# A one-token attention kernel: uniform rolled loops, weights at the front of the DMA queue, and the output weights at its end in 4 KB rows

## The chip, the cores and the metric

The kernel runs on one core of one Trainium2 chip. The metric is the device time of one execution in microseconds (us). A time is the median of its runs.

The profile is one execution recorded by the hardware. PE is the tensor engine (PEld its weight loads), DVE the vector engine, ACT the scalar engine, POOL the general one, and SP the engine that issues DMAs. The profile shows 16 DMA engines, which share each large read: every 4 MB read counts up its semaphore in 16 increments.

## The reference

One query token attends to a cache of 65536 keys; beside it stands a small GELU feed-forward layer. Everything is bf16.

```python
xn  = layernorm(x)                                   # x: [1, 1, 512]
q   = (xn @ wq) -> 32 heads of 128                   # wq: [512, 4096], 4 MB
k,v = caches [8 kv heads, 65536, 128]                # 134 MB each; 4 query heads share one
o   = softmax(q k^T / sqrt(128)) v
out = x + o @ wo + gelu(xn @ w1 + b1) @ w2 + b2      # wo: [4096, 512], 4 MB; w1, w2 1.8 MB each
```

In all 280.5 MB must be read for 1 KB of result.

## The kernel before

K and V are read in 32 units each; a unit is 16384 keys, 4 MB, 32 KB in each of the 128 partitions, and each partition's 32 KB are contiguous in memory. There are four buffers ("slots") of 4 MB, two for K and two for V. For each K unit PE transposes 128 tiles into PSUM, DVE and ACT copy them out, and PE multiplies them with q ("scores"). ACT takes exponentials. PE then multiplies V's 128 tiles with the probabilities ("PV"). SP issues the next read of a slot as soon as PE is done with it. Here are the order of the reads and the emission of the programs; cuts are marked.

```python
chunks = [("K", 0), ("K", 1)]
for u in range(2, NU):
    chunks += [("K", u), ("V", u - 2)]
chunks += [("V", NU - 2), ("V", NU - 1)]
# after K0: four small loads and wq (into a V slot); after K1: w1, w2 (the other V slot)
# the last V goes in four pieces, then the wo rows of the last four heads:
LASTP = (64, 32, 16, 16)
...
def dma_wo_cur(k):            # two heads of wo at a time, one such load in each later pair
    sch.dma(SP, lambda: sp.dma_start(
        out=wo_cur[:, :, :],
        in_=A_wo[k * HW * DH:(k + 1) * HW * DH, :].rearrange("(h p) n -> p h n", p=128)),
        sem_misc, writes=["wo_cur"])        # a row of wo is 512 bf16: 1 KB
...
def pair(i):                  # two units; the first pair has special cases and stands unrolled
    ...
    scores(0, 1)
    v_block(ua - 2, 0)        # PV in four blocks between the scores
    scores(0, 2)
    v_block(ua - 2, 1)
    ...
@block.scalar
def _(e): _emit(e, ACT.ops)   # straight-line program
@block.vector
def _(e): _emit(e, DVE.ops)   # straight-line program
@block.tensor
def _(e): ...                 # PE: first pair straight, the other 15 in a loop, then the tail
```

Of the kernel before, what the change touches and what calls it, by code (L numbers as in the profile page):

```python
# [22 lines left out]
class _Eng:  # L23
    def __init__(self, name, sem, is_pe=False):
        self.name = name
        self.sem = sem
        self.count = 0
        self.clock = {}
        self.ops = []
        self.is_pe = is_pe  # L30
        self.deferred = []

# [11 lines left out]
class _Sched:  # L44
# [61 lines left out]
    def op(self, eng, fn, reads=(), writes=(), publish=True, inc=1):  # L106
        req = self._required(reads, writes)
# [43 lines left out]
def _fold(bodies):  # L151
# [13 lines left out]
    ops = []  # L165
    for k in range(len(bodies[0])):
        assert len({(b[k][2] or (None, 0))[1] for b in bodies}) == 1
        need = {}
        for (kk, s), at in seen.items():
            if kk == k:  # L170
                need[s] = max(v - i * growth[s] for i, v in at.items())
        ops.append((bodies[0][k][1], bodies[0][k][2], need))
    out = []
    known = {}
    for fn, pub, need in ops:
        waits = [(s, v) for s, v in need.items() if known.get(s) is None or known[s] < v]
        for s, v in waits:
            known[s] = v
        out.append((waits, fn, pub))
# [14 lines left out]
def _emit_loop(eng_obj, ops, growth, n):  # L194
# [7 lines left out]
    for s, vs in uses.items():  # L202
        key = (vs[0], growth[s]) if len(vs) == 1 else s
        if key not in regs:
            r = eng_obj.alloc_register(f"w{len(regs)}")
            eng_obj.reg_mov(r, vs[0])
            regs[key] = r
            steps.append((r, vs[0] + growth[s] - vs[-1]))
        at[s] = [regs[key], vs[0]]
    with eng_obj.Fori(0, n):  # L210
# [10 lines left out]
        for r, step in steps:  # L221
            eng_obj.reg_add(r, r, step)


def bass_parallel_sum__gqa_block_cached__dense_activation_gelu__decode_kernel(
# [31 lines left out]
    CW = TPD * HPG  # L257
    assert D % 128 == 0 and F % 128 == 0 and S % CKEYS == 0 and CPG == 4
    assert A_k_cache.shape[3] == DH and H % G == 0 and KT == 4 and HPG == 4
    assert KT * H * DH <= TPD * DH and KT * F + FC * D <= TPD * DH and CW <= 512  # L260

# [18 lines left out]
    ident_bf = nc.alloc_sbuf_tensor("ident_bf", [128, 128], BF)  # L280
    ident_f = nc.alloc_sbuf_tensor("ident_f", [128, 128], F32)
    ones_f = nc.alloc_sbuf_tensor("ones_f", [128, 128], F32)

    rows_bf = nc.alloc_sbuf_tensor("rows_bf", [2, D], BF)
    ones2_bf = nc.alloc_sbuf_tensor("ones2_bf", [2, 1], BF)
    xT_bf = nc.alloc_sbuf_tensor("xT_bf", [128, KT], BF)
    b1T_bf = nc.alloc_sbuf_tensor("b1T_bf", [128, FC], BF)
    xT_f = nc.alloc_sbuf_tensor("xT_f", [128, KT], F32)
    xsq = nc.alloc_sbuf_tensor("xsq", [128, KT], F32)
    st = nc.alloc_sbuf_tensor("st", [128, 2], F32)  # L290
    mom = nc.alloc_sbuf_tensor("mom", [128, 8], F32)
    xnT_bf = nc.alloc_sbuf_tensor("xnT_bf", [128, KT], BF)
    qT_bf = nc.alloc_sbuf_tensor("qT_bf", [128, H], BF)
    q_cur = nc.alloc_sbuf_tensor("q_cur", [128, HPG], BF)
    h_f = nc.alloc_sbuf_tensor("h_f", [128, FC], F32)
    g_t1 = nc.alloc_sbuf_tensor("g_t1", [128, FC], F32)
    g_t2 = nc.alloc_sbuf_tensor("g_t2", [128, FC], F32)
    gT_bf = nc.alloc_sbuf_tensor("gT_bf", [128, FC], BF)
    finT = nc.alloc_sbuf_tensor("finT", [128, KT], F32)
    fin_bf = nc.alloc_sbuf_tensor("fin_bf", [128, 128], BF)  # L300
# [3 lines left out]
    kv = nc.alloc_sbuf_tensor("kv", [128, NSLOT * TPD * DH], BF)  # L304
# [4 lines left out]
    w1_sb = kv[:, w1_at:w1_at + KT * F].rearrange("p (kt f) -> p kt f", kt=KT)  # L309
    w2_at = w1_at + KT * F  # L310
    w2_sb = kv[:, w2_at:w2_at + FC * D].rearrange("p (fc n) -> p fc n", fc=FC)
    kt_ring = nc.alloc_sbuf_tensor("kt_ring", [128, NKT * BCOL], BF)
    HW = 2
    wo_cur = nc.alloc_sbuf_tensor("wo_cur", [128, HW, D], BF)
    HT = HPG + HW
    wo_end = nc.alloc_sbuf_tensor("wo_end", [128, HT, D], BF)
    P_bf = [nc.alloc_sbuf_tensor(f"P_bf{i}", [128, CW], BF) for i in range(2)]
    P_v = [P_bf[i][:, :].rearrange("p (t j) -> p t j", j=HPG) for i in range(2)]

    pmax = nc.alloc_sbuf_tensor("pmax", [128, HPG], F32)  # L320
    gmax4 = nc.alloc_sbuf_tensor("gmax4", [HPG, 1], F32)
    diag4 = nc.alloc_sbuf_tensor("diag4", [HPG, HPG], F32)
    negm = nc.alloc_sbuf_tensor("negm", [128, NU * HPG], F32)
    sums = nc.alloc_sbuf_tensor("sums", [128, NU * HPG], F32)
    o_all = nc.alloc_sbuf_tensor("o_all", [128, NU * HPG], F32)
    nmin = nc.alloc_sbuf_tensor("nmin", [128, H], F32)
    coef = nc.alloc_sbuf_tensor("coef", [128, NU * HPG], F32)
    wtot = nc.alloc_sbuf_tensor("wtot", [128, NU * HPG], F32)
    rden = nc.alloc_sbuf_tensor("rden", [128, H], F32)
    o_c = nc.alloc_sbuf_tensor("o_c", [128, NU * HPG], F32)  # L330
    o_sum = nc.alloc_sbuf_tensor("o_sum", [128, H], F32)
    oT_cur = nc.alloc_sbuf_tensor("oT_cur", [128, HW], BF)
    oT_next = nc.alloc_sbuf_tensor("oT_next", [128, HW], BF)
    sums_cur = nc.alloc_sbuf_tensor("sums_cur", [128, CPG * HPG], F32)
    spare = nc.alloc_sbuf_tensor("spare", [128, 2], F32)
    oL_bf = nc.alloc_sbuf_tensor("oL_bf", [128, HPG], BF)
# [7 lines left out]
    PA_MOM = 48  # L344
    PA_SB = 56
    PA_AT = 72
    PA_FT = 80
# [3 lines left out]
    LASTP = (64, 32, 16, 16)  # L351
    LASTH = (HPG - 1, 1)
    assert sum(LASTP) == TPD
    lsem = [sch.dsem(f"lsem{i}") for i in range(len(LASTP))]
    csem = [sch.dsem(f"csem{i}") for i in range(NSLOT)]
    sem_misc = sch.dsem("dmisc")
    sem_wq = sch.dsem("dwq")
    sem_w12 = sch.dsem("dw12")
    sem_wo = sch.dsem("dwo")
    hsem = [sch.dsem(f"hsem{i}") for i in range(len(LASTH))]  # L360
    sem_out = sch.dsem("dout")


    for t, res in ((wo_cur, "wo_cur"), (oT_next, "oT_next"), (sums_cur, "sums_cur")):
        sch.op(POOL, lambda t=t: pool.memset(t[:], 0.0), writes=[res])
# [11 lines left out]
    sch.op(POOL, lambda: pool.memset(ones2_bf[:, :], 1.0), writes=["ones2"])  # L377


    chunks = [("K", 0), ("K", 1)]  # L380
    for u in range(2, NU):
        chunks += [("K", u), ("V", u - 2)]
    chunks += [("V", NU - 2), ("V", NU - 1)]
    next_chunk = [0]
    slot_free = [True, True, False, False]
    after_chunk = {}

    def slot_of(kind, u):
        if kind == "K":
            return u % 2  # L390
        return NK + u % 2 if u < NU - 2 else (0, NK)[u % 2]

    def issue_chunks():
        while next_chunk[0] < len(chunks):
            kind, u = chunks[next_chunk[0]]
            b = slot_of(kind, u)
# [6 lines left out]
            if (kind, u) == ("V", NU - 1):  # L403
                t0 = 0
                for i, n in enumerate(LASTP):
                    sch.dma(SP, lambda b=b, src=src, t0=t0, n=n: sp.dma_start(  # L406
                        out=slot[b][:, t0:t0 + n, :], in_=src[:, t0:t0 + n, :]),
                        lsem[i], writes=[f"last{i}"] + ([f"slot{b}"] if i == 0 else []))
                    t0 += n
                dma_wo_last()  # L410
            else:
                sch.dma(SP, lambda b=b, src=src: sp.dma_start(out=slot[b], in_=src),
                        csem[b], writes=[f"slot{b}"])
            next_chunk[0] += 1
            for f in after_chunk.get((kind, u), ()):
                f()

    def dma_small():
        for dst, src, res in (
            (xT_bf[:, :], A_x[0, 0].rearrange("(p kt) -> p kt", kt=KT), "xT_bf"),  # L420
            (b1T_bf[:, :], B_b1.rearrange("(p fc) -> p fc", fc=FC), "b1T_bf"),
            (rows_bf[0:1, :], A_x[0], "row0"),
            (rows_bf[1:2, :], B_b2.rearrange("(o n) -> o n", o=1), "row1"),
        ):
            sch.dma(SP, lambda dst=dst, src=src: sp.dma_start(out=dst, in_=src), sem_misc,
                    writes=[res], total=64)

    def dma_wq():
        sch.dma(SP, lambda: sp.dma_start(out=wq_sb, in_=A_wq.rearrange("(p kt) n -> p kt n", kt=KT)),
                sem_wq, writes=[f"slot{NK}"])  # L430

    def dma_w12():
        sch.dma(SP, lambda: sp.dma_start(out=w1_sb, in_=B_w1.rearrange("(p kt) f -> p kt f", kt=KT)),
                sem_w12, writes=[f"slot{NK + 1}", "w1"], total=32)
        sch.dma(SP, lambda: sp.dma_start(out=w2_sb, in_=B_w2.rearrange("(p fc) n -> p fc n", fc=FC)),
                sem_w12, writes=["w2"], total=32)

    def dma_wo_cur(k):
        sch.dma(SP, lambda: sp.dma_start(
            out=wo_cur[:, :, :],  # L440
            in_=A_wo[k * HW * DH:(k + 1) * HW * DH, :].rearrange("(h p) n -> p h n", p=128)),
            sem_misc, writes=["wo_cur"])

    def dma_wo_end():
        sch.dma(SP, lambda: sp.dma_start(
            out=wo_end[:, 0:HW, :],
            in_=A_wo[(H - HT) * DH:(H - HPG) * DH, :].rearrange("(h p) n -> p h n", p=128)),
            sem_wo, writes=["wo_end"])

    def dma_wo_last():  # L450
        h0 = 0
        for i, n in enumerate(LASTH):
# [456 lines left out]
```

## Time and profile before

| | before |
|---|---|
| time, median of 3 runs | 665.35 us (665.21 to 665.43) |
| span of the profiled run | 663.3 us |
| DMA engines busy with data | 99.1% of the span |
| PE, DVE, ACT busy | 84%, 41%, 37% |
| first data packet starts, last one ends | 1.8 us, 660.0 us |

The lines below are from the page of the kernel before: the busy times, the DMA lines of the 40 slices (16.6 us each), and the DMA queues with packets, megabytes and share of the 16 engines' time.

```profile
PE 560.4 (84%) x12846; PEld 529.3 (80%) x12846; DVE 274.0 (41%) x628; ACT 244.5 (37%) x469; POOL 2.3 (0%) x13
...
DMA  9999999999999999999999999999999999999996
GB/s 380 417 433 430 427 426 433 431 427 429 437 428 428 429 429 435 427 429 431 427 433 429 429 429 425 431 427 437 425 429 431 427 437 427 427 425 434 433 421 249
...
q1 hardware_dynamic: 14732, 280.51, 99.1%
q8 instruction: 14, 0.23, 0.1%
q14 instruction: 10, 0.08, 0.0%
```

DMA is the bound. Only the first two slices and the last two are below 425 GB/s. The lines "instruction" are reads of program code, done by the same DMA engines: in this trace eight such loads of 8 KB lie between 100 and 650 us, and behind each of them one 32 KB packet of data took 1.59 to 1.88 us where the median is 1.22 us.

Next are two lines of the page's DMA issues (size of each, median time from issue to landing), and the group of the transposes, whose last columns are PE's idle time before them and its cause.

```profile
kv<-in_A_k_cache_dram SPq DMA_DIRECT2D x32, 4096.0 KB, 28.4
kv<-in_A_v_cache_dram SPq DMA_DIRECT2D x31, 4096.0 KB, 32.3
```

```profile
L499 PE MATMUL pst<-ident_bf,kv 128*128 128x128 bf16 x4096 | 315.8, 246 | 84.2 <-DMA kv<-in_A_k_cache_dram 82.6
```

A 4 MB read takes some 9.8 us when alone at 430 GB/s, yet lands 28 to 32 us after its issue: there are always about two other reads queued before it. So PE waits for DMA (82.6 us in all) and not the other way round.

The end is where DMA time is lost. These are windows of the kernel before; in each line the window, its length, the busy time of PE, PEld, DVE, ACT and POOL, the granted PE clock, the mean busy share of the DMA engines, and GB/s.

```profile
655.00:656.00 1.00, 0.59 (x22) 0.51 (x20) 0.00 (x0) 0.00 (x0) 0.00 (x0) 0.50 0.78 295
656.00:657.00 1.00, 1.00 (x38) 0.92 (x36) 0.00 (x0) 0.00 (x0) 0.00 (x0) 0.50 0.64 242
657.00:658.00 1.00, 0.78 (x29) 0.69 (x27) 0.00 (x0) 0.00 (x0) 0.00 (x0) 0.50 0.55 183
658.00:659.00 1.00, 0.41 (x16) 0.33 (x13) 0.00 (x0) 0.00 (x0) 0.00 (x0) 0.50 0.23 77
659.00:660.00 1.00, 0.58 (x16) 0.50 (x16) 0.23 (x2) 0.00 (x0) 0.00 (x0) 0.50 0.07 23
```

The share falls step by step because the 16 engines end at different times. A share of 0.06 is one engine of sixteen: in the last window one engine alone was working. The semaphores show the same: the 16 increments for the last piece of V came between 654.18 and 659.06 us, and PE's wait for that piece ended at 659.11 us, after the last of them. So the engine that ends last decides.

The packet records in the trace (one for each contiguous row of a read) give the median time of a packet on its engine, over the kernels of this study:

```
bytes    ns    GB/s of one engine
 1024    46 to 51 (51 in e1_wo_1kb)   20.1 to 22.3
 2048    84    24.4
 4096   159 to 164   25.0 to 25.8
 8192   313    26.2
16384   614    26.7
32768  1215    27.0
```

### The profile page before, as it was taken

What the parts mean: (1) busy time and instruction counts of PE and PEld (TensorE: products, weight loads), DVE (VectorE), ACT (ScalarE), POOL (GpSimd) and SP (SyncE); (2) the same over time, 40 slices, a digit from 0 to 9 for tenths busy, and PEclk for the clock granted to TensorE, in tenths of its full rate; (3) what the DMA queues carried; (4) which work ended last, traced back from release to release, by engine and by line L of the source; (5) the groups of instructions that cost most, each with busy time, mean ns of one, the idle gap of its engine ahead of it and who ended that gap; (6) DMA issues with size and microseconds to landing.
All of it is one profiled execution on the core that took longest, in us unless ns stands there. A gap on an engine that the chain in (4) does not pass through costs nothing.

```text
span 663.3 us, 27482 instructions
## 1 busy us (share of the span) xinstructions
PE 560.4 (84%) x12846; PEld 529.3 (80%) x12846; DVE 274.0 (41%) x628; ACT 244.5 (37%) x469; POOL 2.3 (0%) x13
## 2 busy tenths in 40 slices
PE   1799879998887898888799888898888899778896
PEld 1689769898787888887788777888778898777895
DVE  0445324454443444443344443345433354433441
ACT  1354224444332344332344422344423344422340
POOL 1000000000000000000000000000000000000000
PEclk9887668887676788676788667888767888766885
DMA  9999999999999999999999999999999999999996
GB/s 380 417 433 430 427 426 433 431 427 429 437 428 428 429 429 435 427 429 431 427 433 429 429 429 425 431 427 437 425 429 431 427 437 427 427 425 434 433 421 249
DMA packets 14756, 280.82 MB, mean 423 GB/s; under 512 B 1674, under 2 KB 5772, under 8 KB 6028
## 3 DMA queue, kind: packets, MB, share of 16 engines
q1 hardware_dynamic: 14732, 280.51, 99.1%
q8 instruction: 14, 0.23, 0.1%
q14 instruction: 10, 0.08, 0.0%
HBM read 280.50 MB, written 0.00 MB: 423 GB/s over the span
## 4 chain that ended last, share of the span: by engine, by line
DMA 62%; PE 34%; issue 2%; ACT 1%; SPq 0%; DVE 0%
DMA kv<-in_A_k_cache_dram 57%; PE pst L499 25%; DMA wo_end<-in_A_wo_dram 5%; PE pss L519 4%; PE pO L574 2%; PE pA L540 1%; PE pA L550 1%; PE pA L592 1%; PE pA L607 1%; ACT kt_ring L509 0%; PE pA L634 0%; SPq L406 0%; ACT P_bf L560 0%; ACT L560 0%; ACT L484 0%
## 5 line engine op out<-in xcount | busy, mean ns | idle before, releaser
L499 PE MATMUL pst<-ident_bf,kv 128*128 128x128 bf16 x4096 | 315.8, 246 | 84.2 <-DMA kv<-in_A_k_cache_dram 82.6
L499 PEld LDWEIGHTS pst<-ident_bf,kv 128*128 128x128 bf16 x4096 | 287.3, 112 | 103.5 <-DMA kv<-in_A_k_cache_dram 71.4
L509 ACT ACTIVATE kt_ring<-pst 128x1024 bf16<-128x1024 bf16 x192 | 197.8, 1031 | 394.0 <-PE pst L499 391.3
L507 DVE COPY kt_ring<-pst 128x1024 bf16<-128x1024 bf16 x320 | 212.0, 688 | 216.7 <-PE pst L499 216.3
L574 PE MATMUL pO<-P_bf,kv 128*128 128x4 bf16 x4096 | 120.6, 165 | 10.0 <-issue 8.3
L519 PE MATMUL pss<-q_cur,kt_ring 128*128 128x4 bf16 x4096 | 121.3, 164 | 2.0 <-issue 1.5
L574 PEld LDWEIGHTS pO<-P_bf,kv 128*128 128x128 bf16 x4096 | 113.9, 100 | 11.2 <-issue 8.7
L519 PEld LDWEIGHTS pss<-q_cur,kt_ring 128*128 128x128 bf16 x4096 | 116.1, 97 | 2.2 <-issue 1.6
L527 DVE TENSOR_REDUCE pmax<-pss 128x4 f32<-128x512 f32 x32 | 22.1, 692 | 101.8 <-PE pss L519 101.8
L560 ACT ACTIVATE P_bf<-pss,negm 128x128 bf16<-128x128 f32 x128 | 50.8, 552 | 7.6 <-DVE negm L553 7.6
L560 ACT ACTIVATION_READ_ACCUMULATOR P_bf<-pss,negm 128x1 f32 x128 | 36.1, 282 | 0.0
L583 DVE COPY o_all<-pO 128x4 f32<-128x4 f32 x31 | 5.0, 162 | 38.3 <-PE pO L574 38.3
L540 PE MATMUL pA<-ident_f,pmax 128*4 128x128 f32 x64 | 16.9, 362 | 0.3 <-DVE finT L712 0.3
L550 PE MATMUL pA<-diag,ones_f 4*128 4x4 f32 x64 | 12.4, 261 | 0.3 <-DVE finT L712 0.3
L550 PEld LDWEIGHTS pA<-diag,ones_f 4*128 4x128 f32 x64 | 9.6, 186 | 3.6 <-DVE finT L712 0.3
L542 DVE TENSOR_REDUCE gmax<-pA 4x1 f32<-4x128 f32 x32 | 8.6, 269 | 0.7 <-PE pA L540 0.7
L540 PEld LDWEIGHTS pA<-ident_f,pmax 128*4 128x4 f32 x64 | 2.9, 84 | 6.0 <-DVE kt_ring L507 5.3
L544 DVE TENSOR_SCALAR diag<-ident_f,gmax 4x4 f32<-4x4 f32 x32 | 7.0, 217 | 1.1
L677 PE MATMUL pA<-sums_cur,ones_f 128*128 128x16 f32 x32 | 6.2, 270 | 0.0
L553 DVE TENSOR_SCALAR negm<-pA 128x4 f32<-128x4 f32 x32 | 5.1, 160 | 0.7 <-PE pA L550 0.7
L707 PE MATMUL pA<-oT_cur,wo_cur 128*128 128x1 bf16 x120 | 5.3, 165 | 0.0
L592 PE MATMUL pA<-xnT_bf,kv 128*128 128x1 bf16 x128 | 3.5, 164 | 1.8 <-DVE xnT_bf L487 1.8
(74 smaller groups left out, 62.2 us busy)
## 6 DMA issues: line engine op xcount, KB each, us to landing
kv<-in_A_k_cache_dram SPq DMA_DIRECT2D x32, 4096.0 KB, 28.4
kv<-in_A_v_cache_dram SPq DMA_DIRECT2D x31, 4096.0 KB, 32.3
kv<-in_A_wq_dram SPq DMA_DIRECT2D x1, 4096.0 KB, 20.1
kv<-in_B_w_dram SPq DMA_DIRECT2D x2, 1792.0 KB, 36.5
wo_cur<-in_A_wo_dram SPq DMA_DIRECT2D x13, 256.0 KB
kv<-in_A_v_cache_dram SPq DMA_DIRECT2D x1, 2048.0 KB, 27.5
kv<-in_A_v_cache_dram SPq DMA_DIRECT2D x1, 1024.0 KB, 29.6
kv<-in_A_v_cache_dram SPq DMA_DIRECT2D x2, 512.0 KB, 30.8
```

Of the source, the lines that this page charges most:

```text
L499: lambda tb=tb, at=at, b=b, tt=s * TPB + t: pe.transpose(pst[tb][:, at * 128:(at + 1) * 128], slot[b][:, tt, :], ident_bf[:, :]),
L507: e, fn = DVE, lambda tb=tb, dst=dst: dve.tensor_copy(out=dst, in_=pst[tb][:, :])
L509: e, fn = ACT, lambda tb=tb, dst=dst: act.activation(out=dst, in_=pst[tb][:, :], func=ACTF.Copy)
L519: lambda k=k, kb=kb, at=at, t=t: pe.matmul(pss[k][:, at:at + HPG], lhsT=kt_ring[:, kb * BCOL + t * 128:kb * BCOL + (t + 1) * 128], rhs=q_c ...
L527: lambda k=k: dve.tensor_reduce(out=pmax[:, :], in_=pss[k][:, 0:CW].rearrange("p (t j) -> p j t", j=HPG), axis=AX.X, op=ALU.max),
L540: sch.op(PE, lambda: pe.matmul(pA[0:HPG, PA_ST:PA_ST + 128], lhsT=pmax[:, 0:HPG], rhs=ident_f[:, :], start=True, stop=True), reads=["pmax" ...
L542: sch.op(DVE, lambda: dve.tensor_reduce(out=gmax4[:, :], in_=pA[0:HPG, PA_ST:PA_ST + 128], axis=AX.X, op=ALU.max), reads=["pA"], writes=[" ...
L544: sch.op(DVE, lambda: dve.tensor_scalar(out=diag4[:, :], in0=ident_f[0:HPG, 0:HPG], scalar1=gmax4[0:HPG, 0:1], scalar2=None, op0=ALU.mult) ...
L550: sch.op(PE, lambda: pe.matmul(pA[:, PA_SB:PA_SB + HPG], lhsT=ones_f[0:HPG, 0:128], rhs=diag4[0:HPG, 0:HPG], start=True, stop=True), reads ...
L560: lambda k=k, u=u, j=j, src=src: act.activation(out=P_v[k][:, :, j], in_=src[:, :, j], func=ACTF.Exp, bias=negm[:, u * HPG + j:u * HPG + j ...
L574: lambda k=k, b=b, t=t: pe.matmul(pO[:, 0:HPG], lhsT=slot[b][:, t, :], rhs=P_v[k][:, t, :], start=t == 0, stop=t == TPD - 1),
L592: lambda h=h, kt=kt: pe.matmul(pA[:, PA_Q + h:PA_Q + h + 1], lhsT=wq_sb[:, kt, h * DH:(h + 1) * DH], rhs=xnT_bf[:, kt:kt + 1], start=kt == ...
```

## The change

Its intent: every unit is treated alike, so that PE, DVE and ACT all run in loops; the weights come first; PV runs one and a half units behind its scores, as one block at the start of a half of the loop; and wo comes last, mostly in 4 KB rows, while PE still works on the last units. The diff is cut to its core.

```diff
-    for u in range(2, NU):
-        chunks += [("K", u), ("V", u - 2)]
-    chunks += [("V", NU - 2), ("V", NU - 1)]
+    for u in range(2, NU):
+        chunks += [("V", u - 2), ("K", u)]
+    chunks += [("V", NU - 2), ("V", NU - 1), ("W", 0)]
...
-    (V31 in four pieces; wo in 14 loads of two heads beside the V's; the last four heads last)
+    def dma_wo():            # 28 heads: each partition takes 4 successive rows of wo
+        ... out=wo_sb[:, g0:g0 + n].rearrange("p g r n -> p g (r n)"),
+            in_=A_wo[...].rearrange("(g p r) n -> p g (r n)", p=128, r=HPG)
+        ... last 4 heads: in_=A_wo[...].rearrange("(h p) n -> p h n", p=128)   # 1 KB rows
+    dma_small(); dma_wq(); dma_w12(); issue_chunks()
...
-    pA[:, h] += wq_sb[:, kt, head h].T @ xnT[:, kt]     # 128 matmuls, weights stationary
+    pss[b][32*j, :] += xnT[:, kt].T @ wq_sb[:, kt, 512 columns]   # 32 matmuls, weights moving
+    (the rows are then turned into columns by small matmuls; w1 and w2 likewise)
...
+    def half(i, b):
+        u = 2 * i + b
+        pv(u - 2)                       # for units -2 and -1: zero probabilities, frees wq's, w2's slot
+        transposes(b, 0); stats_1(); transposes(b, 1); stats_2(u - 1)
+        transposes(b, 2); scores(b, 0); transposes(b, 3); done_chunk("K", u)
+        scores(b, 1); ...; scores(b, 2); scores(b, 3)
...
-    _emit(e, ACT.ops)            /  _emit(e, DVE.ops)
+    _emit_rolled(e, ACT.ops, ...) / _emit_rolled(e, DVE.ops, ..., group)
...
+    the tail: stats, pv(30), regroup o for the 4 KB rows (16 small matmuls), pv(31),
+    then 112 matmuls for 28 heads of wo and 16 for the last four
```

## The prediction

> **What bounds it now.** The DMA queue. The page gives PE 84% busy, DVE 41%, ACT 37%, but the DMA engines 99.1%, and every slice between the first two and the last two moves 425-437 GB/s. [...] 280.5 MB must move whatever the order. The queue never runs dry: a K chunk lands 28.4 us after its issue, a V chunk 32.3 us (DMA issues), while its own transfer takes 9.8 us, so 18 to 22 us of other work lies before it. PE waits about 85 us in all for K.
>
> Only the ends leave DMA time: the first packet starts at 1.8 us; from 654 us the windows fall to 333, 213 and 50 GB/s because the 16 engines finish between 655.4 and 660.0 us (mean about 657.3); then come 16 matmuls (0.6 us), the cast (0.3 us) and the 2.0 us store.
>
> **What the change moves.**
> - wo, 4096 rows of 1 KB: a 1 KB packet takes 47 ns on its engine, a 4 KB one 164 ns (packet records). 4096x47/16 = 12.0 us now; 896x164/16 + 512x47/16 = 10.7 us after: -1.3 us.
> - The last V goes as one piece in 32 KB rows: 9.8 us instead of 10.5: -0.7 us.
> - Instruction loads: ACT's and DVE's straight-line programs and PE's first pair shrink into loops. 24 loads of 8 or 16 KB take 0.1% of the engines now; perhaps half goes: -0.3 us.
> - Weights first: wq, w1, w2, K0, K1 are queued without a wait, so DMA has work to about 41 us. PE finishes projections, FFN and dummy PV by about 30 us, so V0 is issued in time. PE saves about 5 us of matmuls, worth nothing.
> - PV as one block before its half's transposes: the same 128+128+128 matmuls and evacuations per chunk. PE needs about 17 us of the 19.6 us per chunk pair; K is issued some 18 us and V some 22 us before DMA reaches it (estimate from the durations of before). No DMA idle time appears or goes.
> - [...]
> - wo last: its 10.7 us follow the last V. That V's PV (3.6 us) and the 64 matmuls of the first wo piece hide under it; 48 wait for the second piece, which lands about 1.6 us before the end, and at 37 ns each (16 took 0.60 us) need 1.8 us. PE ends 0.5 to 1 us after the last landing instead of 0.6: +0.2 us.
>
> **On the critical path:** -1.3 -0.7 -0.3 +0.2 = -2.1 us, perhaps -3 if fewer instruction loads shorten the slowest engine's list, which alone decides the last landing. PE's, ACT's and DVE's changes are off it.
>
> **Prediction:** 663.0 us, 660.8 to 665.3. Faster by over 2%: 0.01; within 2%: 0.96; slower by over 2%: 0.03.
>
> **What would show it.** Right: slices stay at 425-437 GB/s to the end of V; no dip at 40-50 us; the last wo lands near 658 us; the chain ends in DMA of wo, 4 to 20 small matmuls, cast, store; 896 wo packets near 164 ns. Wrong: slices under 420 GB/s in mid-run, PE idle for ACT or DVE growing, many wo matmuls after the last landing.
>
> **What would make it wrong.** Register waits that slow the evacuations until PE needs over 19.6 us per chunk pair. A late V0 or K2 (DMA gap near 40 us). Wo matmuls near 100 ns instead of 37 (+3 us). A final spread of the 16 engines that differs by 2 us either way.

## The result, and the profile after

| | before | after |
|---|---|---|
| time, medians of the first comparison | 665.38 us | 661.63 us (661.35 to 661.84, 4 runs) |
| ratio | | 0.9944 (0.9927 to 0.9961) |
| the same on another chip, 5 rounds | 665.36 us | 661.66 us, ratio 0.9947 |
| span of the profiled run | 663.3 us | 659.8 us |
| first packet starts, last packet ends | 1.8, 660.01 us | 1.8, 656.27 us |
| last packet's end to the end of the span | 3.3 us | 3.5 us |

The whole gain of 3.7 us is in the time of the last landing. The forecast of 663.0 us, 660.8 to 665.3, holds, but the gain is 3.7 us where 2.3 us were forecast (665.35 to 663.0 us; its listed terms add to 2.1 us). First the same lines of the page of the changed kernel:

```profile
PE 567.6 (86%) x12957; PEld 530.4 (80%) x12957; DVE 279.4 (42%) x616; ACT 244.9 (37%) x470; POOL 4.2 (1%) x19
...
DMA  9999999999999999999999999999999999999996
GB/s 369 441 426 433 420 436 423 443 425 435 431 427 439 429 435 428 429 435 425 441 427 433 431 427 437 431 435 429 429 437 425 441 425 433 433 425 437 431 428 251
...
q1 hardware_dynamic: 11128, 280.50, 99.1%
q8 instruction: 10, 0.16, 0.1%
...
q14 instruction: 2, 0.02, 0.0%
```

DMA is busy as before and still the bound. No slice in the middle falls below 420 GB/s. The loads on q14 fell from 10 to 2. The DMA issues and the transposes' group of the changed kernel follow:

```profile
kv<-in_A_k_cache_dram SPq DMA_DIRECT2D x32, 4096.0 KB, 27.5
kv<-in_A_v_cache_dram SPq DMA_DIRECT2D x32, 4096.0 KB, 30.7
```

```profile
L569 PE MATMUL pst<-ident_bf,kv 128*128 128x128 bf16 x4096 | 313.3, 245 | 49.6 <-DMA kv<-in_A_k_cache_dram 49.3
```

The queue is as deep as before. PE still waits for K, though less. The next lines are the start of SP's timeline of the changed kernel, which shows that V0 and K2 were issued at 29.9 and 43.7 us:

```profile
2.13 1.21 SPq L426 DMA_DIRECT2D kv<-in_A_k_cache_dram  x2
29.89 0.33 SPq L426 DMA_DIRECT2D kv<-in_A_v_cache_dram  x1
43.70 0.33 SPq L426 DMA_DIRECT2D kv<-in_A_k_cache_dram  x1
```

The forecast had "about 30 us" for V0, 11 us before the queue would run dry. Last, the windows of the end, and PE's timeline there (start, length, engine, line, operation, count; in brackets idle time and its cause, where "issue" stands for a wait for nothing that the profile shows):

```profile
653.00:654.00 1.00, 0.30 (x12) 0.01 (x2) 0.00 (x0) 0.00 (x0) 0.00 (x0) 0.50 0.68 227
654.00:655.00 1.00, 0.00 (x0) 0.00 (x0) 0.00 (x0) 0.00 (x0) 0.00 (x0) 0.50 0.29 87
655.00:656.00 1.00, 0.64 (x21) 0.56 (x25) 0.00 (x0) 0.00 (x0) 0.00 (x0) 0.50 0.11 36
656.00:657.00 1.00, 1.00 (x51) 1.00 (x43) 0.00 (x0) 0.00 (x0) 0.00 (x0) 0.50 0.08 22
```

```profile
641.51 3.57 PE L649 MATMUL pO<-P_bf,kv 128*128 128x4 bf16 x128
...
646.82 2.11 PE L649 MATMUL pO<-P_bf,kv 128*128 128x4 bf16 x73
649.45 1.61 PE L649 MATMUL pO<-P_bf,kv 128*128 128x4 bf16 x55 [0.52 <-issue]
...
651.37 1.93 PE L773 MATMUL pss<-kv,oX_bf 128*1 128x128 bf16 x64
655.36 1.61 PE L773 MATMUL pss<-kv,oX_bf 128*1 128x128 bf16 x48 [2.06 <-DMA kv<-in_A_wo_dram]
656.66 0.74 PE L773 MATMUL pss<-kv,oT_last 128*1 128x128 bf16 x16
```

PE is ahead of the second piece of wo by only 2.06 us. That is all the slack that PE has at the end, and two experiments below run into it.

The windows also tell how much of the gain is the last engine's alone. Their shares add up to a mean end of the sixteen engines near 657.3 us before (655 and 2.27) and near 654.2 us after (653 and 1.16). So about 3.1 of the 3.7 us are common to all engines, and about 0.6 us are the last one's.

### The profile page after: what moved, and what is told of

Its sections match the earlier page's. It is cut to its first block, busy times and chain, and to the rows that moved or that the text cites. A ratio compares the mean times of both kernels' runs of the same rounds, so it can differ in the third digit from the quotient of the medians.

```text
span 659.8 us, 28552 instructions
## 1 busy us (share of the span) xinstructions
PE 567.6 (86%) x12957; PEld 530.4 (80%) x12957; DVE 279.4 (42%) x616; ACT 244.9 (37%) x470; POOL 4.2 (1%) x19
## 3 DMA queue, kind: packets, MB, share of 16 engines
q1 hardware_dynamic: 11128, 280.50, 99.1%
## 4 chain that ended last, share of the span: by engine, by line
DMA 59%; PE 38%; issue 1%; DVE 1%; SPq 0%; DVEq 0%
DMA kv<-in_A_k_cache_dram 55%; PE pst L569 27%; DMA kv<-in_A_wo_dram 5%; PE pss L589 5%; PE pO L649 4%; PE pA L614 1%; PE pA L625 1%; DVE pmax L597 0%; PE pss L773 0%; DVE kt_ring L577 0%; PE pA L678 0%; SPq L450 0%; SPq L459 0%; SPq L447 0%; SPq L443 0%
## 5 line engine op out<-in xcount | busy, mean ns | idle before, releaser
L649 PEld LDWEIGHTS pO<-P_bf,kv 128*128 128x128 bf16 x4352 | 118.0, 103 | 19.1 <-DVE pmax L597 13.1
L589 PE MATMUL pss<-q_cur,kt_ring 128*128 128x4 bf16 x4096 | 114.1, 164 | 2.4 <-issue 2.4
L589 PEld LDWEIGHTS pss<-q_cur,kt_ring 128*128 128x128 bf16 x4096 | 111.8, 96 | 2.5 <-issue 2.5
L636 ACT ACTIVATE P_bf<-pss,negm 128x128 bf16<-128x128 f32 x132 | 52.5, 553 | 4.0 <-DVE negm L628 4.0
L500 PE MATMUL pA<-ones_bf,xn_row 1*128 1x1 bf16 x4 | 0.3, 174 | 10.5 <-DVE xn_row L496 10.5
L500 PEld LDWEIGHTS pA<-ones_bf,xn_row 1*128 1x128 bf16 x4 | 0.2, 116 | 10.5 <-DVE xn_row L496 10.5
L678 PEld LDWEIGHTS pA<-sums_cur,ones_f 128*128 128x128 f32 x34 | 5.3, 195 | 2.2 <-DVE sums_cur L672 2.2
```

The lines of the kernel that those rows point to most:

```text
L589: lambda k=k, kb=kb, at=at, t=t: pe.matmul(pss[k][:, at:at + HPG], lhsT=kt_ring[:, kb * BCOL + t * 128:kb * BCOL + (t + 1) * 128], rhs=q_c ...
L636: lambda k=k, at=at, j=j, src=src: act.activation(out=P_v[k][:, :, j], in_=src[:, :, j], func=ACTF.Exp, bias=negm[:, at:at + 1], scale=1.0 ...
L649: lambda k=k, b=b, t=t: pe.matmul(pO[:, 0:HPG], lhsT=slot[b][:, t, :], rhs=P_v[k][:, t, :], start=t == 0, stop=t == TPD - 1),
L678: sch.op(PE, lambda: pe.matmul(pA[:, PA_SUM:PA_SUM + GW], lhsT=ones_f[:, :], rhs=sums_cur[:, :], start=True, stop=True), reads=["ones_f", ...
```

## The experiments

The theory at this point (A): the gain is the sum of the DMA work saved, counted by packet records. With the forecast it gives 2.3 us. Three rivals for the missing 1.4 us: short rows cost more than their records (B); code loads delay one DMA engine each, and only delay on the last engine counts (C); the small wo transfers between the chunks cost extra (D). Each run was timed against the kernel before on the same chip; the base is the changed kernel run again. All runs computed the right result.

| run | time, us | against 661.66 | kernel before, same rounds | ratio to it |
|---|---|---|---|---|
| r0_after_again | 661.66 | | 665.36 | 0.9947 |
| e1_wo_1kb | 663.01 | +1.35 | 665.36 | 0.9965 |
| e2_straight | 662.97 | +1.31 | 665.36 | 0.9962 |
| e3_vsplit | 661.70 | +0.04 | 665.36 | 0.9945 |
| e10_dve_straight | 663.29 | +1.63 | 665.43 | 0.9966 |
| e7_three | 664.46 | +2.80 | 665.30 | 0.9988 |
| e8_spread | 670.40 | +8.74 | 665.35 | 1.0076 |
| e4_kfirst | 676.20 | +14.54 | 665.35 | 1.0160 |
| e5_pe32 | 664.93 | +3.27 | 665.35 | 0.9987 |
| e6_pe128 | 921.85 | +260 | 665.30 | 1.3856 |
| e9_long_rows | 661.05 | -0.61 | 665.35 | 0.9934 |
| e11_best | 660.71 | -0.95 | 665.43 | 0.9929 |

The runs lie on four chips; the kernel before differed by at most 0.13 us between them, so differences of a few tenths mean little across rows.

**r0_after_again**: the changed kernel unaltered.

> The changed kernel unaltered, as the base for its neighbours on this chip. Both theories: about 661.6 us, 3.7 us under the kernel before.

It came out as expected.

**e1_wo_1kb**: wo of the first 28 heads in 1 KB rows, in the same place.

```diff
-   in_=A_wo[...].rearrange("(g p r) n -> p g (r n)", p=128, r=HPG)
+   in_=A_wo[...].rearrange("(h p) n -> p h n", p=128)
-   fin_mm(kt, oX_bf[:, r, g:g + 1], wo_sb...)
+   fin_mm(kt, oT_all[:, (g + 1) * HPG + r:(g + 1) * HPG + r + 1], wo_sb...)
```

> The changed kernel with the first 28 heads of wo read in 1 KB rows at the same place, at the end. Theory A (a row costs what its packet record says, 47 ns for 1 KB against 164 ns for 4 KB): 3584 packets more cost 3584x(47-41)/16 = 1.3 us, so about 662.9 us. Rival B (the extra gain of 1.4 us over my forecast came from short rows costing more than their records): 2 us or more, over 663.6 us.

It cost 1.35 us (five runs, 662.84 to 663.49). Theory A's figure came out, and B falls. The match is not exact, though: the profile is of the slowest of the five runs, and in it the 1 KB packets took 51 ns and not the 47 ns that A assumes, so that by its records wo cost 2.3 us more. It has the last packet at 658.08 us instead of 656.09 us in the base run. The table of packets above shows the same in kind: 4 KB took 164 ns as one packet, and as four of 1 KB at 46 ns they take 184 ns.

**e2_straight**: the ACT and DVE programs written out again.

```diff
-   _emit_rolled(e, ACT.ops, ...)          # and DVE
+   _emit(e, ACT.ops)                      # DVE: the same, with the group index set while emitting
```

> The changed kernel with the ACT and DVE programs written out straight, as before; PE stays in its loop. Theory A (forecast: half of the instruction loads, 0.3 us): +0.3 us, about 661.9 us, with some 8 loads of 8 KB back in mid-run. Rival C (each load delays one engine that is already the slowest, so that the loads are the missing 1.4 us): +1 to +1.5 us.

It cost 1.31 us: theory A's 0.3 us fails, C's figure fits. By the records, eight loads of 8 KB lie between 60 us and the end of the data where the base has one, and the summed time of all data packets over 16 engines grew by only 0.4 us. The last packet, though, ended at 657.93 us instead of 656.09 us. PE is late as well in this run: the transposes of its last K start at 628.74 us instead of 625.45 us, for PE waits until a read's last engine is done (in the kernel before, above, the last increment came at 659.06 us and PE went on at 659.11 us). The 112 matmuls of wo then run without a wait:

```profile
654.99 3.47 PE L782 MATMUL pss<-kv,oX_bf 128*1 128x128 bf16 x112
```

So PE and the data end together here. The next run, in which PE still waits for wo (0.69 us), is the cleaner one.

**e10_dve_straight**: the same for DVE alone, to tell whether a load costs its share of the bandwidth or delays one engine.

```diff
-   _emit_rolled(e, DVE.ops, ...)
+   _emit_flat(e, DVE.ops, ...)            # ACT and PE stay in loops
```

> The changed kernel with only the DVE program written out straight; ACT and PE stay in loops. With both straight the time rose by 1.3 us. Theory C (a load of program code delays just the one DMA engine that fetches it, and only delay on the engine that finishes last counts): one of the two programs carries it nearly all, so either +1.0 us or more (about 662.8 us, then it is DVE's loads) or +0.3 us or less (about 661.8 us, then it is ACT's). Theory A (each load takes its share of the whole bandwidth): about half, +0.5 to +0.8 us, and the last landing moves by no more than the mean one.

DVE alone costs 1.63 us, no less than both. So ACT's loads cost nothing that can be seen and DVE's everything, which a share of bandwidth can't do. The windows of this run show the mechanism; read the share and GB/s at the end of each line.

```profile
653.00:654.00 1.00, 1.00 (x40) 0.95 (x40) 0.03 (x1) 0.00 (x0) 0.00 (x0) 0.50 0.66 234
654.00:655.00 1.00, 1.00 (x37) 0.90 (x33) 0.66 (x4) 0.00 (x0) 0.00 (x0) 0.50 0.38 124
655.00:656.00 1.00, 1.00 (x45) 0.89 (x36) 0.00 (x0) 0.00 (x0) 0.00 (x0) 0.50 0.06 25
656.00:657.00 1.00, 0.31 (x9) 0.08 (x1) 0.00 (x0) 0.00 (x0) 0.00 (x0) 0.50 0.07 25
657.00:658.00 1.00, 0.98 (x37) 0.85 (x40) 0.00 (x0) 0.00 (x0) 0.00 (x0) 0.50 0.05 16
```

Fifteen engines are done before 654.8 us, about when they are done in the changed kernel. One works on alone until 657.74 us, at 25 GB/s. The mid-run code loads of DVE begin at 181, 309, 450 and 588 us and take 0.33 us each; behind each of them one 32 KB packet takes 1.87 us instead of 1.22 us. A load thus costs its engine about 1.0 us. The records do not name the engine, but it can be followed: on one engine a packet starts some 3 ns before the one before it ends (3 to 4 ns is the most frequent overlap in the traces of both kernels). All four stretched packets lie on one engine. It ended its share of a read 1.1 us behind the mean of the sixteen before 309 us, 2.0 us after it, 2.9 us after 450 us and 3.8 us after 588 us; in the base run no engine is over 1.2 us behind after 100 us.

Of the 2.8 us more, the last landing shows 1.65 us, because the base run has another last engine. There a 16 KB load of PE's code for the tail runs from 652.50 to 653.60 us. At its end begins a row of packets of one engine, the first two 4 KB ones slow (441 and 347 ns), that goes on without a gap to the last packet at 656.09 us; the other fifteen engines are done by 654.7 us. In e2_straight, ACT's loads (at 248, 418 and 583 us) stretch a packet each to 1.59 us, but they lie together on another engine than DVE's, and the last one is not later for it.

**e3_vsplit**: the last V in four pieces.

```diff
-   sp.dma_start(out=slot[b], in_=src)
+   for n in (64, 32, 16, 16): sp.dma_start(out=slot[b][:, t0:t0 + n, :], in_=src[:, t0:t0 + n, :])
```

> The changed kernel with the last V read in four pieces of 64, 32, 16 and 16 tiles, as before. Theory A: the DMA work grows by 0.7 us (10.5 instead of 9.8 us), so about 662.3 us; PE starts its last PV earlier, which hides under wo and gains nothing.

It cost 0.04 us, which is nothing within the spread. My 10.5 us for the pieces used mean packet times of 662 ns for 16 KB and 322 ns for 8 KB, and those means held slow code loads of the same sizes (1.02 to 1.14 us for 16 KB in the kernel before). Clean medians give 10.0 us, 0.3 us more than one piece, too little to be seen in a spread of 0.6 us.

**e7_three**: e1, e2 and e3 together.

> The changed kernel with three parts undone together: wo in 1 KB rows at the end, ACT and DVE straight, the last V in four pieces. Theory A: the three single costs add, 1.3+0.3+0.7 us, about 663.9 us; what is left to the kernel before (665.4 us) is then the spreading of wo over the run.

It cost 2.80 us; the single costs add to 2.70 us. So they are additive within the spread, and 0.84 us to the kernel before (665.30 us) remain.

**e8_spread**: wo read as before, in 14 loads of 256 KB between the chunks, with the last V in pieces.

```diff
+   if kind == "V" and u % 2 and 3 <= u < NU - 1:      # after V3, V5, ... V29
+       sp.dma_start(out=wo_far[:, 2 * k:2 * k + 2, :], in_=A_wo[256 rows].rearrange("(h p) n -> p h n", p=128))
-   wo in dma_wo() but for the last four heads;  its 112 matmuls after pv(31)
+   the 112 matmuls before pv(31)
```

> The changed kernel with wo read as before: 1 KB rows, 14 transfers of 256 KB spread over the V chunks into a buffer of their own, only the last four heads at the end, and the last V in four pieces. Order of weights, PV place and rolled loops stay. Theory A (only packet records count): +1.3 for the rows, +0.7 for V, -0.2 for the tail, so about 663.4 us. Rival D (a small transfer costs more between chunks than its packets: the stretch from K wait to K wait is 39.8 us before and 38.9 us after, 0.96 us longer for 256 packets of 1 KB where 0.75 us of records were added): 14 times 0.2 us more, about 664.5 to 666 us.

It missed both expectations: 670.4 us. But the last packet ended at 656.61 us, 0.34 us after the changed kernel's and 1.47 us before e1's. That is the last engine alone, however. The summed time of all data packets over 16 engines is 2.6 us above the base run's, where the rows and the pieces of V account for 1.6 us. Another 0.8 us stand on 234 packets of 32 KB that took 16 to 85 ns longer than 1215 ns, 224 of them within 3 us of a spread packet of wo. The kernel before has 241 such packets (0.8 us), the changed kernel 10. So D's cost exists, but at some 0.06 us and not 0.2 us for each transfer. Most of the time was lost after the landing, on PE; its timeline:

```profile
636.05 3.59 PE L583 MATMUL pst<-ident_bf,kv 128*128 128x128 bf16 x32 [3.00 <-DMA kv<-in_A_k_cache_dram]
...
652.09 3.57 PE L663 MATMUL pO<-P_bf,kv 128*128 128x4 bf16 x128
...
657.70 3.20 PE L784 MATMUL pss<-wo_far,oT_all 128*1 128x128 bf16 x112
660.83 3.42 PE L663 MATMUL pO<-P_bf,kv 128*128 128x4 bf16 x128
665.12 0.60 PE L784 MATMUL pss<-kv,oT_last 128*1 128x128 bf16 x16 [0.88 <-DVE oT_last L710]
```

From the landing of the last K (its first transpose at 636.05 us) PE needs 29.7 us, with its short waits for DVE, to the last matmul, and DMA has only V30, V31 and 0.5 MB left, about 20.6 us. In the changed kernel the last K's transposes start at 625.46 us: the 3.7 MB of wo stand behind the last K, and PE works off its tail beneath them. The kernel before had the same cover from a third V behind its last K (K31, V29, V30, V31). So "wo last" does not merely move bytes: it replaces the V that the new order took from there. My forecast counted it as +0.2 us and did not see what it protects.

**e4_kfirst**: K0 and K1 queued ahead of the weights.

```diff
-   dma_small(); dma_wq(); dma_w12(); issue_chunks()
+   dma_small(); issue_chunks(); dma_wq(); dma_w12()
```

> The changed kernel with K0 and K1 queued ahead of the weights. Its PE still does the projections and the dummy PV first, so V0 can only be issued when w2 has landed (about 41 us) and PE has done FFN and dummy PV (about 48 us). Theory A (queue order at the start matters only through the first slot that comes free): DMA idles some 7 to 9 us near 41 us, so 669 to 671 us. If instead the time stays at 661.6 us, the weights' place is free.

It cost 14.5 us, more than the 7 to 9 us expected. Windows of this run:

```profile
40.00:44.00 4.00, 2.44 (x22) 1.30 (x22) 1.05 (x6) 0.22 (x1) 0.00 (x0) 0.88 0.03 11
44.00:48.00 4.00, 3.21 (x99) 2.65 (x98) 0.69 (x1) 0.00 (x0) 0.00 (x0) 0.50 0.02 4
48.00:52.00 4.00, 4.00 (x68) 4.00 (x66) 1.23 (x3) 1.02 (x1) 0.00 (x0) 0.50 0.60 176
...
60.00:64.00 4.00, 3.33 (x119) 3.16 (x116) 1.16 (x5) 1.13 (x2) 0.00 (x0) 0.94 0.81 285
```

The first gap is as expected: V0 was issued at 49.03 us. But then the queue had no depth, and K2, V1 and K3 were issued (60.0, 69.6 and 80.6 us) just as DMA ran dry, so that windows fell below full rate again until about 90 us. Of these two orders, only the one with the weights first keeps DMA busy under the uniform loops.

**e5_pe32**: 32 extra matmuls in every PV block.

```diff
+   for t in range(32):  pe.matmul(pO[:, 64:68], lhsT=slot[b][:, t, :], rhs=P_v[k][:, t, :], start=True, stop=True)
```

> The changed kernel with 32 extra matmuls in each PV block (34 blocks, about 0.9 us each, 30 us of PE work in all). Theory A (PE is off the critical path, with 1.7 us to spare in each half of 19.4 us): under 0.5 us more, about 661.6 to 662.1 us, and PE's wait for K falls from 49 us to about 20 us. If PE bounds any stage: up to 30 us more.

It cost 3.27 us (four runs, 663.38 to 665.25), so the expectation of under 0.5 us failed, but not in mid-run. The last packet ended at 656.37 us, as in the changed kernel, with PE's wait for K down to 23.3 us: 30 us more of PE work moved no landing. At the end, where the slack is 2.06 us, PE came late:

```profile
649.03 0.27 PE L654 MATMUL pO<-P_bf,kv 128*128 128x4 bf16 x5 [1.91 <-issue]
...
655.24 1.61 PE L654 MATMUL pO<-P_bf,kv 128*128 128x4 bf16 x55 [1.24 <-issue]
...
657.16 3.25 PE L778 MATMUL pss<-kv,oX_bf 128*1 128x128 bf16 x112
```

All 112 matmuls of wo now run without a wait, after the data. Not all of the delay is the extra matmuls: the waits marked "issue" grew from 0.56 us in the base run to 3.15 us, each near a 16 KB load of PE's code (ending at 647.61 and 653.93 us). That PE waited for its own code there is likely, but not shown. "Off the critical path" was true for the loop and not for the tail.

**e6_pe128**: 128 instead of 32 extra matmuls.

> The changed kernel with 128 extra matmuls in each PV block (about 3.5 us each). Theory A: PE then needs 17.7+3.5 = 21.2 us in a half where DMA needs 19.4 us; PE becomes the bound and 32 halves cost about 1.8 us each: some 715 to 725 us, with DMA slices near 395 GB/s.

It took 921.85 us, far beyond the 715 to 725 us expected. These are its q8 line on the page, and its group of the extra matmuls:

```profile
q8 instruction: 149, 2.44, 1.0%
```

```profile
L647 PE MATMUL pO<-P_bf,kv 128*128 128x4 bf16 x4352 | 125.3, 166 | 158.3 <-issue 157.5
```

There were 149 loads of 16 KB instead of 10, some nine more for each of the loop's 16 rounds, so PE's program was loaded again and again, and PE stood 157.5 us before the extra matmuls with nothing else to wait for. Each matmul comes with a weight load of its own (the page of the changed kernel lists 12957 of either). A round of the loop has 768 large matmuls in the changed kernel (10 loads in all), 832 with 32 extra in each half (11 loads) and 1024 with 128 (149 loads). Where between 832 and 1024 it turns, and why, no run shows. As a measure of PE's slack this run failed; it shows that this loop must not grow to 1024 matmuls a round.

**e9_long_rows**: the whole wo in rows of 16, 10, 4 and 2 KB.

```diff
-   28 heads "(g p r) n", 4 heads "(h p) n"
+   for n in (16, 10, 4, 2):  in_=A_wo.rearrange("(p r) n -> p r n", p=128)[:, r0:r0 + n, :]
+   # row p*32+r: o is spread into a [128, 4*128] tile with zeros and regrouped by 4 matmuls with the identity
```

> A version meant to beat both: the whole wo in rows of 16, 10, 4 and 2 KB (each partition takes 32 successive rows of wo; the attention output is regrouped by four small matmuls while wo loads). Theory A: DMA work for wo falls from 10.7 to about 10.0 us, so about 660.9 us, with PE ending 0.3 to 0.5 us after the last landing.

It took 661.05 us, 0.6 us less, in runs from 660.63 to 662.02 us; the profile is of the slowest. The last packet ended at 655.79 us, but PE's last matmul only at 657.81 us: every wo matmul now waits for the last PV, and PE bounds the end.

**e11_best**: e9, and the last but one PV between the steps of the last statistics.

```diff
-   stats_1(); stats_2(L); pv(L - 1)
+   pv(L - 1, 0..47); stats_1(); pv(L - 1, 48..95); stats_2(L); pv(L - 1, 96..127)
```

> The long rows of wo and, besides, the last but one PV block placed between the steps of the last statistics, where PE stood idle for 2.3 us. In the run with long rows PE ended about 1.3 us after it saw the last piece land, so PE bounded that end. Theory: PE starts its last PV about 1.2 us sooner (V has landed by then), the wo matmuls end 0.5 us after the last landing is seen, and the time falls by 0.6 to 0.9 us against long rows alone, to about 660.3 us. Rival: if the landing of wo alone bounds the end, it stays at 661.0 us.

It took 660.71 us (660.60 to 660.83), 0.34 us less than e9 where 0.6 to 0.9 us were expected. That lies within e9's own spread, so a gain over e9 is not shown. PE's timeline at its end:

```profile
645.86 3.57 PE L643 MATMUL pO<-P_bf,kv 128*128 128x4 bf16 x128
...
651.10 1.88 PE L764 MATMUL pss<-kv,oX_bf 128*1 128x128 bf16 x64 [0.28 <-DVE oX_bf L780]
654.14 2.29 PE L764 MATMUL pss<-kv,oX_bf 128*1 128x128 bf16 x64 [1.16 <-DMA kv<-in_A_wo_dram]
```

PE waits for wo again, so DMA is the bound to the end. This version beats both kernels: ratio 0.9929 to the kernel before, and 0.95 us below the changed one (medians of different rounds, with the kernel before within 0.07 us).

## Why the prediction was right or wrong

- **The bound was read rightly.** DMA stayed at 99.1%, and the gain is the last landing's: 660.01 to 656.27 us. That PE's saved matmuls at the start and the new place of PV moved nothing is not shown by a run of their own; what they did move is in the open 0.84 us below. The chance of 0.96 for "within 2%" and the range held, the range partly by luck: it was 4.5 us wide, and the 0.7 us counted too much for V made up for part of what was counted too little for the loads.
- **wo in 4 KB rows, -1.3 us:** right in time. Undone, it costs 1.35 us.
- **Weights first:** right. V0 was issued at 29.89 us for a forecast of about 30 us, and there was no dip. Undoing the order showed that it is needed (+14.5 us), not that it gains.
- **The end of PE, +0.2 us:** right in size, 3.3 to 3.5 us after the last packet. Incomplete in kind: wo at the end also covers PE's 30 us of tail work.
- **The last V in one piece, -0.7 us:** wrong size; 0.04 us by experiment and 0.3 us by clean packet records. The mean packet times were polluted by code loads of the same sizes.
- **Instruction loads, -0.3 us:** this step was mis-sized most. Undone, it costs 1.31 us, with DVE's loads alone 1.63 us. I had spread the loads over 16 engines. In fact a load delayed one engine, by about 0.7 us (ACT's: 0.31 us and a packet of 1.59 for 1.22 us) or 1.0 us (DVE's: 0.33 us and 1.87 for 1.22 us), and in e10_dve_straight all four of DVE's mid-run loads fell on the same one. In the kernel before, too, one engine was 2.1 us behind the mean before DVE's load at 588 us and 3.0 us after it. The forecast named this in half a sentence ("perhaps -3 if fewer instruction loads shorten the slowest engine's list") but did not price it: -1.35 -1.31 -0.04 is -2.7 us, measured together -2.8 us. These are prices from the changed kernel, and not the only way to split the gain: by the records the summed packet time over 16 engines fell by 3.6 us (wo 1.3, the last V 0.3, the other 32 KB packets 1.5, small ones the rest), so that the forecast's way of counting comes near the whole gain once nothing is left out.
- **Still open: 0.84 us** between the three undone together and the kernel before. By the records the summed packet time of e7_three is 0.9 us below that of the kernel before. Candidates that no run separates are the fewer early loads of PE's code (12 after 20 us in the kernel before, 6 after, apart from single later ones), the small transfers spread over the run (0.8 us on the 32 KB packets beside them, but then 47 and not 51 ns for a 1 KB packet), and the rest of the start. In both kernels, too, the last 0.7 to 1.4 us belong to a single engine. In the changed kernel it is the one that the load of PE's tail code held up; no run removed that load.

## What to carry to other kernels

Here DMA was busy to the end (99.1% of the span), and the time followed the work of all DMA engines (3.1 of the 3.7 us) and how far the last one was behind them (0.6 us; in e10_dve_straight, 1.63 us slower, one worked alone for the last 3 us). Where a profile looks like this, look at the last windows' share in sixteenths. Reads of program code ride on those engines: 0.0% in the queue table cost 1.3 us here, and rolling DVE's program into a loop removed it; but watch the loads when a PE loop grows (a round of 832 matmuls was not loaded again, 11 loads; one of 1024 was, 149 loads and 260 us more). Before you move a transfer in the queue, ask which engine's remaining work it covers; what stands behind the last K is the time that PE has for its tail.
